# Single-block weight pieces and another order of scratch tiles in a fused mLSTM and SwiGLU kernel

## The chip, the cores and the metric

The kernel runs on one core of one Trainium2 chip. The metric is the time of one execution in microseconds (us), as the device reports it; the number that counts is the median of several runs. A core has a matmul engine (PE), a vector engine (DVE), a scalar engine for activations (ACT), a general engine (POOL), and SP, which here only issues DMAs. Each engine works through its own queue in order; semaphores hold an instruction until what it needs is there. DMAs that SP issues run on queue q1, those that POOL issues on queue q0; both move data through the same 16 DMA engines.

## What is computed

The reference has two steps. The first is an mLSTM cell over 768 time steps for 4 x 8 heads of 40 features; the second is a SwiGLU block on the 3072 x 320 matrix that the first gives.

```python
for t in range(S):
    m_new = np.maximum(f_gate[:, :, t] + m, i_gate[:, :, t])
    f_stab = np.exp(f_gate[:, :, t] + m - m_new); i_stab = np.exp(i_gate[:, :, t] - m_new)
    C = f_stab * C + i_stab * (v_t outer k_t);  n = f_stab * n + i_stab * k_t
    y[:, :, t] = sigmoid(o_gate) * (C @ q_t) / max(|n . q_t|, 1)
x = y as (3072, 320)
g = x @ w_gate;  out = (g * sigmoid(g) * (x @ w_val)) @ w_out
```

The three weight matrices come as 64-bit floats (320 x 1536, 320 x 1536 and 1536 x 320); all else is 32-bit. No engine of the kernel works in 64 bits, so the kernel turns the weights into 32-bit floats by integer operations on their two halves.

## The kernel before

**Tiling.** Time is cut into 6 groups of 128 steps (`g` from 0 to 5). For each group the recurrence is written in its chunked form: scores `k` against `q` (`sp`), weights from the gates (`w_sb`), the part from inside the chunk (`intra`), the part from the state (`inter`), and the update of the state (`add`, `C`). The group's output `x` (512 tokens of 320 features) is turned so that features lie on the partitions (`xT`), and the SwiGLU block follows for those tokens. The 1536 hidden features are 12 blocks of 128, so the two first matrices are 12 blocks each; block m of both is kept in `wgv_sb[:, m]`, gate weights on partitions 0 to 63 and value weights on partitions 64 to 127.

**Group 0** does a plain product for each block (`hidden`, L741 to L755: 40 matmuls of 512 columns at L749, then Silu on ACT and a multiplication on DVE at L755) and a plain output projection (`project_all`). **Groups 1 to 5** use a seven-product scheme for both matrix products: `gated` (L892 to L954) needs sums of weight blocks (`weight_sums`, L869 to L877, into the tiles `sw0` and `sw` and into `wgv_sb` itself) and sums of `xT` (`input_sums`); `project_seven` needs `wT`, `S1` and `S2`. The sums of weights are made once, in group 1.

**The weights come in while group 0 runs.** `PIECES` (L162) lists the loads: for `gv` (gate and value) or `o` (output matrix), the first block and the number of blocks. `piece_load` (L166 to L203) issues for a `gv` piece three DMAs: the gate half from SP, and the value half in two parts from POOL (`parts` 0, and 1 and 2; GATE and VALUE at L644). The 64-bit words land in a raw buffer: the pool `conv` has two buffers `raw` of 10,240 bytes per partition; some pieces take a home elsewhere that is free just then, the end of `h_sb` (`raw_h`, L645) or `wo_sb`. A piece that takes a `raw` buffer again waits until ACT has read the former piece. Then each block is converted (`convert`, L252): `scale` on ACT (two instructions, `top` at L225 and `low` at L227), `join` on DVE (L234, L235) and `rounded` on POOL or DVE (L242). Only then can PE use the block at L749.

**Before**, the `gv` pieces are: block 0, block 1, then pairs (2,3), (4,5), (6,7), (8,9), (10,11). Pieces 0 and 1 share one `raw` buffer; piece 2 lies in `raw_h`; piece 3 in the other `raw`; piece 5 in `wo_sb`. The tail of `h_sb` has held the first inputs (`dense`, L257). A memset of one element on POOL (L693) stands before piece 2, so that its DMAs wait for POOL alone.

**The order of the work** is written out by hand. L646 to L709 is the start: the first chunk's scores and weights, the turning of `x` (`seam`), the loads of pieces 0 to 3, and the conversion of blocks 0, 1 and 2. From L1011 on, lists say what follows which block of group 0: `ahead` (which block is converted while block m is multiplied), `slots` (what is issued after block m), `amid`, and `after` (what follows block m of the output projection of group 0). What stands in these lists is issued in that order on each engine's queue. The steps that matter here: in `slots`, 0 holds the loads of the next two pieces, 3 holds the load of the second group's `q` (`load_all` L1004, `load` L139, on SP), 5 the load of blocks 10 and 11 and of `v`; in `after`, 5 converts the last block, 6 and 7 make the weights of the third group (`weights_bias`, 16 exponentials each on ACT at L533) and weigh the values with them (`weigh_values`, L394 on POOL), 8 clears `x_sq` (POOL, L1008), 10 and 11 update the state (`do_decayed` on POOL at L418, `do_add` on PE at L409, `do_state` on DVE at L425) and turn `k` from a `raw` buffer (`early_squares(1)`, `turn_squares`, L373 on DVE). Group 1 then loads the next `k` into `x_sq` (`load_squares`, L367 on SP).

**Memory.** After group 0, the pools `early` and `conv` are closed (L1058) and the pool `late` takes their place: `wT` (11,520 bytes per partition), `S1` and `S2` (6,144 each) and `sw` (13,312), one behind the other in this order (L1066 to L1069). A late tile waits for the last use of the tiles that it lies over. By the sizes in the code, `early` fills about the first 6.6 KB of that space, then come the two `raw` buffers of 10,240 bytes, `top` and two `low`.

Of the kernel before, what the change touches and what calls it, by code (L numbers as in the profile page):

```python
# [9 lines left out]
F32 = mybir.dt.float32  # L10
BF16 = mybir.dt.bfloat16
I32 = mybir.dt.int32
U32 = mybir.dt.uint32
# [11 lines left out]
def kernel(  # L25
# [18 lines left out]
    nc = tc.nc  # L44
# [9 lines left out]
    NFC = DF // 128  # L54
# [3 lines left out]
    NKC = DM // HP  # L58
# [15 lines left out]
    def flat(t):  # L74
        return t.rearrange("p c t -> p (c t)")
# [44 lines left out]
    wo_sb = const.tile([128, NFC, DM], F32)  # L120
# [7 lines left out]
    x_sq = const.tile([128, B * NKC, L // SQ, SQ], F32)  # L128
# [30 lines left out]


    raws = {}
    PIECES = [("gv", 0, 1), ("gv", 1, 1)] + [("gv", m, 2) for m in range(2, NFC, 2)] + [("o", m, 4) for m in range(0, NFC, 4)]  # L162

    homes = {}

    def piece_load(p, home=None, parts=(0, 1, 2)):  # L166
        kind, m, n = PIECES[p]
        if kind == "gv":
            a, d = NKC, n * 128
            gate_w, val_w = (w[:, m * 128:(m + n) * 128].rearrange("(c p) f -> p c f", p=HP) for w in (moe_w_gate, moe_w_val))  # L170
            src = [(slice(0, HP), slice(0, NKC), gate_w), (slice(HP, 128), slice(0, NKC - 1), val_w[:, 1:]),
                   (slice(HP, 128), slice(NKC - 1, NKC), val_w[:, 0:1])]
        else:
            a, d = n, DM
            src = [(slice(0, 128), slice(0, n), moe_w_out[m * 128:(m + n) * 128].rearrange("(a p) d -> p a d", p=128))]
        if src[0][2].dtype == F32:
            for r, cs, w in [src[x] for x in parts if x < len(src)]:
                if kind == "o":
                    nc.sync.dma_start(out=wo_sb[r, m:m + n, :], in_=w)
                else:  # L180
                    for x in range(n):
                        nc.sync.dma_start(out=wgv_sb[r, m + x, cs], in_=w[:, :, ts(x, 128)])
            return
        if p in homes:
            raw = homes[p]
        else:
            if p < 2:
                if p == 0:
                    homes["raw"] = conv.tile([128, 4 * NKC * 128], U32, name="raw")
                raw = homes["raw"][:, ds(2 * p * a * d, 2 * a * d)]  # L190
            elif home is None:
                raw = conv.tile([128, 4 * NKC * 128], U32, name="raw")
            else:
                raw = home.rearrange("p a t -> p (a t)").bitcast(U32)
# [25 lines left out]
    def scale(j):  # L220
        if j in blocks:
            lo, hi, dst = blocks[j]
            a, d = hi.shape[1], hi.shape[2]
            top = conv.tile([128, NKC * 128], F32, name="top", bufs=1).rearrange("p (a d) -> p a d", a=a)
            nc.scalar.mul(top, hi.bitcast(F32), 2.0 ** -112)  # L225
# [335 lines left out]
    A, V, G = nc.scalar, nc.vector, nc.gpsimd  # L561
# [82 lines left out]
    GATE, VALUE = (0,), (1, 2)  # L644
    raw_h = h_sb[:, NH - NKC:]  # L645
# [38 lines left out]
    first_scores(1)  # L684
    first_gate(0, (G, G), A)
    piece_load(1, parts=VALUE)
    first_own(2)
    first_x(2)
    first_own(3)
    first_x(3)  # L690
    seam(0, 0, (A, A, A, A))
    first_gate(1, (G, V), V)
    nc.gpsimd.memset(raw_h[:, 0, 0:1], 0.0)  # L693
    piece_load(2, raw_h)
    piece_load(3)
    scale(0)
    ps0 = first_state(0, "gen")
    seam(0, 1, (V, A, A, A))
# [74 lines left out]
    KH = NFC // 2  # L773
# [230 lines left out]
    def load_all(dst, a, n, eng=nc.sync):  # L1004
        for P in range(2):
# [5 lines left out]
    on_vector = (9, 10, 11)  # L1011
    ahead = {0: [], 1: [3], 2: [4], 3: [5], 4: [6], 5: [7], 6: [8], 7: [9], 8: [10], 9: [11], 10: [], 11: []}
    slots = {
        0: [run(piece_load, 4), run(piece_load, 5, wo_sb)],
        1: [run(late_sums)],
        2: [run(late_maxima), run(M_store, G), run(load_all, k_sb, k, 1)],
        3: [run(late_decay), run(weights_load, 1), run(load_all, q_sb, q, 1)],
        4: [run(nc.scalar.activation, step1, step1, AF.Exp), run(decay_rows), run(cap_table)],
        5: [run(piece_load, 6), run(load_all, v_sb, v, 1), run(late_turns), run(decay)],
        6: [run(turn_one, P, k_sb, kT, (A, A)) for P in range(2)] + [run(weights_cap, 0), run(weights_cap, 1), run(piece_load, 7)],  # L1020
        7: [run(weights_sub, 1, 0), run(weights_sub, 1, 1), run(weights_exp, 0), run(weights_exp, 1), run(weigh_values, G, 0),
            run(weigh_values, G, 1)],
        8: [run(nc.gpsimd.memset, q_sb, 0.0), run(do_scores), run(piece_load, 8), run(load_all, o_sb, o_gate, 1)],
        9: [run(do_weigh, 0), run(do_weigh, 1), run(do_decayed, 2)],
        10: [run(do_add, 1, (0,)), run(rounded, 12), run(load_squares, q_sq, q, 2, (0,))],
        11: [run(do_intra, 0), run(do_inter, 1, 0), run(do_gather, 1, 0, False), run(piece_load, 9),
             run(load_squares, q_sq, q, 2, (1,))],
    }
    amid = {8: [run(turn_one, P, q_sb, qT, (A, A)) for P in range(2)], 11: [run(do_add, 1, (1,)), run(do_state, 2)]}
# [6 lines left out]
    def early_squares(part):  # L1036
# [11 lines left out]
        3: [run(do_divide, 1, 1), run(weights_cap, 0)],  # L1048
        4: [run(seam, 1, 0, (A, A, A, A)), run(convert, 16), run(weights_cap, 1), run(turn_squares, q_sq, qT)],
        5: [run(seam, 1, 1, (A, A, A, A)), run(convert, 17)],  # L1050
        6: [run(weights_bias, 2, 0), run(weigh_values, G, 0), run(input_sums, V)],
        7: [run(weights_bias, 2, 1), run(weigh_values, G, 1)],
        8: [run(nc.gpsimd.memset, x_sq, 0.0)],
        10: [run(do_decayed, 4), run(weight_sums, 0, V)],
        11: [run(do_add, 2), run(do_state, 4), run(early_squares, 1)],
    }
# [95 lines left out]
```

## Time and profile before

| | us |
|---|---|
| median of 3 runs (lowest, highest) | 514.84 (513.79, 519.25) |
| the profiled execution | 514.3 |
| its span, first to last instruction | 511.9 |
| PE busy | 502.5 (98% of the span) |
| DVE, POOL, ACT busy | 333.9, 261.9, 208.4 |
| DMA, mean over the span | 85 GB/s; 0 to 60 us: 192 GB/s |

The profile is of one execution. The page gives sums for each engine, a chain of work that ended last, and groups of instructions; the trace behind it can be asked for the waits of an engine, for all instructions in a stretch of time, and for the DMAs issued in a stretch. Times are from the start of the span. Group 0 takes about the first 126 us, each later group 78 us, and the last one ends without new recurrence work. Matmuls overlap in the pipeline, so the start of the next one says more than the end of the last.

### The profile page before, as it was taken

Reading aid. Unit: us, or ns where it says so; the run is one execution under the profiler, and the core shown is the slowest. Engines: PE = TensorE matmul, PEld = TensorE weight load, DVE = VectorE, ACT = ScalarE, POOL = GpSimd, SP = SyncE. Lnnn points to the kernel's source line nnn. Section 1 sums busy time; section 2 is a strip of 40 time slices with the busy share of each in tenths; the row PEclk is TensorE's granted clock in tenths of the full one; section 3 lists DMA queues with packets and bytes.
Section 4 is the critical chain, followed back from the end, with each engine's and each line's share of the span. In section 5 each row is a group of like instructions: output and inputs, shape, how many; then the busy total and the mean of one; then the engine's idle time right before and its main releaser. Section 6 shows DMA issues by size and latency. Waiting matters only on the chain.

```text
span 511.9 us, 15075 instructions
## 1 busy us (share of the span) xinstructions
PE 502.5 (98%) x6437; PEld 428.4 (84%) x6437; DVE 333.9 (65%) x543; ACT 208.4 (41%) x404; POOL 261.9 (51%) x289
## 2 busy tenths in 40 slices
PE   8989999999899999999999999999999999999997
PEld 4846655667788899888899988899988899988896
DVE  5869768887897777687466578467558554233421
ACT  3664784457342348312339321338321340223210
POOL 3624515366689653367643357652447650166710
PEclk9999999999999999999999999999999999999999
DMA  9999998797702992501992501992101200000001
GB/s 144 187 250 217 158 183 229 150 171 111 98 9 41 173 116 40 80 3 33 170 117 38 89 8 25 163 131 38 42 3 19 37 2 27 27 1 0 1 14 38
DMA packets 184378, 43.29 MB, mean 85 GB/s; under 512 B 172952, under 2 KB 179496, under 8 KB 183672
## 3 DMA queue, kind: packets, MB, share of 16 engines
q1 hardware_dynamic: 182948, 38.26, 46.9%
q0 software_dynamic: 1232, 4.02, 3.3%
q8 instruction: 50, 0.82, 0.7%
q14 instruction: 16, 0.13, 0.1%
q10 hardware_dynamic: 132, 0.07, 0.0%
HBM read 35.68 MB, written 4.01 MB: 78 GB/s over the span
## 4 chain that ended last, share of the span: by engine, by line
PE 85%; ACT 5%; DVE 3%; POOL 2%; issue 2%; DMA 1%; SPq 1%; DVEq 0%; ACTq 0%; POOLq 0%
PE gv_x L899 24%; PE o_ps L820 22%; PE gv_y L899 20%; PE gv_ps L749 6%; PE o_ps L766 3%; PE inter L432 2%; PE intra L441 2%; ACT w_sb L533 2%; PE add L409 1%; PE sp L383 1%; SPq L367 1%; DMA h_sb<-in_moe_w_val_dram 1%; ACT h_sb L582 1%; DVE wgv_sb L235 1%; PE burn L545 1%
## 5 line engine op out<-in xcount | busy, mean ns | idle before, releaser
L899 PE MATMUL gv_x<-xT,wgv_sb 64*128 64x256 f32 x720 | 89.3, 377 | 0.0
L899 PEld LDWEIGHTS gv_x<-xT,wgv_sb 64*128 64x128 f32 x720 | 69.7, 187 | 7.9 <-issue 0.2
L820 PE MATMUL o_ps<-wo_sb,h_sb 128*128 128x160 f32 x480 | 67.4, 300 | 0.0
L820 PEld LDWEIGHTS o_ps<-wo_sb,h_sb 128*128 128x128 f32 x480 | 65.6, 190 | 1.7 <-issue 1.7
L947 ACT ACTIVATE h_sb<-gv_x 128x256 f32<-128x256 f32 x30 | 11.5, 383 | 115.8 <-PE gv_x L899 115.8
L749 PE MATMUL gv_ps<-xT,wgv_sb 64*128 64x512 f32 x240 | 54.3, 597 | 1.5 <-DVE wgv_sb L242 1.4
L749 PEld LDWEIGHTS gv_ps<-xT,wgv_sb 64*128 64x128 f32 x240 | 28.2, 187 | 22.5 <-issue 15.2
L899 PE MATMUL gv_y<-xT,wgv_sb 64*128 64x256 f32 x360 | 44.0, 376 | 0.0
L899 PE MATMUL gv_y<-q_sb,wgv_sb 64*128 64x256 f32 x360 | 44.0, 376 | 0.0
L394 POOL TENSOR_TENSOR vw_sb<-v_sb,w_sb 128x656 f32<-128x656 f32 x10 | 14.6, 1462 | 53.8 <-ACT w_sb L533 40.5
L899 PEld LDWEIGHTS gv_y<-xT,wgv_sb 64*128 64x128 f32 x360 | 35.0, 187 | 3.9
L899 PEld LDWEIGHTS gv_y<-q_sb,wgv_sb 64*128 64x128 f32 x360 | 35.1, 187 | 3.9
L820 PE MATMUL o_ps<-wT,S 128*128 128x160 f32 x240 | 33.4, 299 | 0.0
L820 PEld LDWEIGHTS o_ps<-wT,S 128*128 128x128 f32 x240 | 32.9, 190 | 0.0
L899 PE MATMUL gv_x<-q_sb,sw 64*128 64x256 f32 x240 | 31.1, 377 | 1.3 <-POOL sw L873 1.3
L533 ACT ACTIVATE w_sb<-w_sb,g_T 128x64 f32<-128x64 f32 x128 | 31.0, 333 | 0.0
L920 POOL TENSOR_TENSOR h_sb<-x_sb 128x512 f32<-128x512 f32 x12 | 15.8, 1313 | 24.6 <-ACT x_sb L919 24.6
L940 POOL TENSOR_TENSOR tmp<-tmp 128x512 f32<-128x512 f32 x15 | 20.1, 1342 | 15.0 <-DVE tmp L939 15.0
L920 POOL TENSOR_TENSOR h_sb<-tmp 128x512 f32<-128x512 f32 x13 | 16.5, 1271 | 21.5 <-ACT tmp L919 21.5
L787 POOL TENSOR_TENSOR S<-h_sb 128x256 f32<-128x256 f32 x30 | 22.7, 756 | 9.2 <-DVE h_sb L920 7.3
L766 PE MATMUL o_ps<-wo_sb,h_sb 128*128 128x320 f32 x96 | 27.2, 438 | 0.0
L899 PE MATMUL gv_y<-q_sb,sw 64*128 64x256 f32 x200 | 27.0, 388 | 0.2 <-DVE tmp L917 0.2
(225 smaller groups left out, 987.2 us busy)
## 6 DMA issues: line engine op xcount, KB each, us to landing
w_sb<-M_dram SPq DMA_DIRECT2D x10, 512.0 KB, 7.2
v_sb<-in_v_dram SPq DMA_DIRECT2D x12, 320.0 KB, 6.2
o_sb<-in_o_gate_dram SPq DMA_DIRECT2D x12, 320.0 KB, 6.4
raw<-in_moe_w_out_dram SPq DMA_DIRECT2D x3, 1280.0 KB, 7.4
k_sb<-in_k_dram SPq DMA_DIRECT2D x10, 320.0 KB, 7.9
x_sq<-k_sb SPq DMA_DIRECT2D x64, 40.0 KB, 3.1
q_sb<-in_q_dram SPq DMA_DIRECT2D x32, 64.0 KB, 3.3
raw<-in_moe_w_gate_dram SPq DMA_DIRECT2D x3, 640.0 KB, 14.3
```

Source lines behind the costliest of these rows:

```text
L394: eng.tensor_tensor(vw_sb[:, heads(P)], v_sb[:, heads(P)], w_sb[:, heads(P), last].to_broadcast([128, UH, D1]), op=ALU.mult)
L432: nc.tensor.matmul(inter[two][half(i), a, :], lhsT=qT[feats(two), P * UA + a, half(i)], rhs=state(2 * n + i)[feats(two), P * UA + a, :], s ...
L441: nc.tensor.matmul(intra[i][half(c), a, :], lhsT=w_sb[half(i), h, :], rhs=v_sb[half(i), h, :], start=True, stop=True)
L533: nc.scalar.activation(w_sb[:, h], w_sb[:, h], AF.Exp, bias=g_T[:, n, h:h + 1], scale=-1.0)
L749: nc.tensor.matmul(ps[i], lhsT=wgv_sb[half(i), m, kc, :], rhs=x[half(i), kc, :], start=(kc == 0), stop=(kc == NKC - 1))
L766: nc.tensor.matmul(ps[u], lhsT=hid(g, m)[:, ts(u, L)], rhs=wo_sb[:, m, :], start=(m == 0), stop=(m == NFC - 1))
L787: eng.tensor_tensor(S1[:, k], lo[:, second_half], hi[:, second_half], op=ALU.add)
L820: nc.tensor.matmul(node[x][:, i], lhsT=lhs(k)[:, ts(i, L)], rhs=rhs(k), start=start and k == 0 and i == 0, stop=stop and k == KH - 1, skip ...
L899: nc.tensor.matmul(ps[:, i, cols], lhsT=lhs(c)[half(i)], rhs=rhs(c)[half(i)], start=start and c == 0, stop=stop and c == n - 1, skip_group ...
L920: (nc.vector if k == KH - 1 else nc.gpsimd).tensor_tensor(h_sb[:, 2 * k + 1], uw[:, 0], uw[:, 1], op=ALU.mult)
L940: nc.gpsimd.tensor_tensor(uw[:, :, second_half], uw[:, :, second_half], uw[:, :, first_half], op=ALU.add)
L947: nc.scalar.activation(h[:, first_half], x[:, 0, first_half], AF.Silu)
```

## The change

Four edits, with no change to what is computed.

1. Blocks 2 and 3 become pieces of one block each. Both lie in `raw_h`, in its two halves, each with a memset of one element of its own. The first memset moves up to stand behind the value request of block 1, ahead of `first_gate(1, ...)`; the second stands between the loads of the two pieces. Blocks 4 and 5 are thus piece 4, and the numbers of all later pieces grow by one. Each piece's request order is gate (SP), then value (POOL).
2. Of blocks 10 and 11, the gate half is still requested in slot 5; the value half moves to the head of slot 6. Slot 3, before both, holds the load of `q`.
3. In `late`, `sw` is allocated first and `wT` last.
4. The memset of `x_sq` moves from `after[8]` to the head of `after[6]`.

```diff
-    PIECES = [("gv", 0, 1), ("gv", 1, 1)] + [("gv", m, 2) for m in range(2, NFC, 2)] + [("o", m, 4) for m in range(0, NFC, 4)]
+    PIECES = [("gv", m, 1) for m in range(4)] + [("gv", m, 2) for m in range(4, NFC, 2)] + [("o", m, 4) for m in range(0, NFC, 4)]
...
-            if p < 2:
+            if p < 4:
                 if p == 0:
                     homes["raw"] = conv.tile([128, 4 * NKC * 128], U32, name="raw")
-                raw = homes["raw"][:, ds(2 * p * a * d, 2 * a * d)]
+                base = homes["raw"] if p < 2 else raw_h.rearrange("p m t -> p (m t)").bitcast(U32)
+                raw = base[:, ds(2 * (p % 2) * a * d, 2 * a * d)]
...
     piece_load(1, parts=VALUE)
+    nc.gpsimd.memset(raw_h[:, 0, 0:1], 0.0)
...
     first_gate(1, (G, V), V)
-    nc.gpsimd.memset(raw_h[:, 0, 0:1], 0.0)
-    piece_load(2, raw_h)
+    piece_load(2)
+    nc.gpsimd.memset(flat(raw_h)[:, 2 * NKC * 128:2 * NKC * 128 + 1], 0.0)
     piece_load(3)
+    piece_load(4)
...
-        0: [run(piece_load, 4), run(piece_load, 5, wo_sb)],
+        0: [run(piece_load, 5), run(piece_load, 6, wo_sb)],
...
-        5: [run(piece_load, 6), run(load_all, v_sb, v, 1), run(late_turns), run(decay)],
-        6: [run(turn_one, P, k_sb, kT, (A, A)) for P in range(2)] + [..., run(piece_load, 7)],
+        5: [run(piece_load, 7, parts=GATE), run(load_all, v_sb, v, 1), run(late_turns), run(decay)],
+        6: [run(piece_load, 7, parts=VALUE)] + [run(turn_one, P, k_sb, kT, (A, A)) for P in range(2)] + [..., run(piece_load, 8)],
...
-        6: [run(weights_bias, 2, 0), run(weigh_values, G, 0), run(input_sums, V)],
+        6: [run(nc.gpsimd.memset, x_sq, 0.0), run(weights_bias, 2, 0), run(weigh_values, G, 0), run(input_sums, V)],
         7: [run(weights_bias, 2, 1), run(weigh_values, G, 1)],
-        8: [run(nc.gpsimd.memset, x_sq, 0.0)],
...
-    wT = late.tile([128, 3, KH, NW], F32, name="wT")
+    sw = late.tile([128, 3 * KH - 5, 2, 128], F32, name="sw")
     S1 = late.tile([128, KH, TH], F32, name="S1")
     S2 = late.tile([128, KH, TH], F32, name="S2")
-    sw = late.tile([128, 3 * KH - 5, 2, 128], F32, name="sw")
+    wT = late.tile([128, 3, KH, NW], F32, name="wT")
```

The loads of the output matrix in slots 8 and 11 only take their new numbers (9 and 10).

More of the change, by code (lines that the diff above doesn't have):

```diff
@@ L1018 @@
         4: [run(nc.scalar.activation, step1, step1, AF.Exp), run(decay_rows), run(cap_table)],
-        5: [run(piece_load, 6), run(load_all, v_sb, v, 1), run(late_turns), run(decay)],
-        6: [run(turn_one, P, k_sb, kT, (A, A)) for P in range(2)] + [run(weights_cap, 0), run(weights_cap, 1), run(piece_load, 7)],
+        5: [run(piece_load, 7, parts=GATE), run(load_all, v_sb, v, 1), run(late_turns), run(decay)],
+        6: [run(piece_load, 7, parts=VALUE)] + [run(turn_one, P, k_sb, kT, (A, A)) for P in range(2)] + [run(weights_cap, 0), run(weights_cap, 1), run(piece_load, 8)],
         7: [run(weights_sub, 1, 0), run(weights_sub, 1, 1), run(weights_exp, 0), run(weights_exp, 1), run(weigh_values, G, 0),
             run(weigh_values, G, 1)],
-        8: [run(nc.gpsimd.memset, q_sb, 0.0), run(do_scores), run(piece_load, 8), run(load_all, o_sb, o_gate, 1)],
+        8: [run(nc.gpsimd.memset, q_sb, 0.0), run(do_scores), run(piece_load, 9), run(load_all, o_sb, o_gate, 1)],
         9: [run(do_weigh, 0), run(do_weigh, 1), run(do_decayed, 2)],
         10: [run(do_add, 1, (0,)), run(rounded, 12), run(load_squares, q_sq, q, 2, (0,))],
-        11: [run(do_intra, 0), run(do_inter, 1, 0), run(do_gather, 1, 0, False), run(piece_load, 9),
+        11: [run(do_intra, 0), run(do_inter, 1, 0), run(do_gather, 1, 0, False), run(piece_load, 10),
              run(load_squares, q_sq, q, 2, (1,))],
```

## The prediction

> **What bounds the kernel now.** I read the page's first two parts, then who waits for whom on the matmul engine, then the stretches of the timeline around those waits, then the DMA queues in the same stretches.
>
> ```profile
> span 511.9 us, 15075 instructions
> PE 502.5 (98%) x6437; PEld 428.4 (84%) x6437; DVE 333.9 (65%) x543; ACT 208.4 (41%) x404; POOL 261.9 (51%) x289
> PEclk9999999999999999999999999999999999999999
> ```
> PE (matmul) is busy 502.5 of 511.9 us at full granted clock. The change neither adds nor removes a matmul, so only PE's 9.4 us of idle time can move, and part of that lies at the start (1.2 us) and after the last matmul (511.9 - 508.0 = about 3.9 us).
>
> ```profile
> PE gv_ps L749 <- DVE wgv_sb L242: 1.4, 1, 1.4
> PE gv_x L899 <- POOL sw L873: 1.3, 1, 1.3
> PE add L409 <- DVE w_sb L390: 0.3, 1, 0.3
> PE tp_x L506 <- POOL x_sb L473: 0.2, 1, 0.2
> PE gv_y L899 <- DVE tmp L917: 0.2, 1, 0.2
> ```
> Columns: total us, times, longest. Two waits of over 1 us are left, both single events. After 139 us PE has no gap that a wait explains.
>
> First wait, block 2's weights (columns: start, length, engine, line, ... idle before):
>
> ```profile
> 34.86 0.79 ACT L225 ACTIVATE top<-h_sb 128x640 f32<-128x640 f32 x1 [3.83 <-DMA h_sb<-in_moe_w_val_dram]
> 37.17 0.82 DVE L242 CUSTOM_DVE_ANT_0 wgv_sb<-wgv_sb,low 128x1280 uint16<-128x1280 uint16 x1
> 38.14 7.21 PE L749 MATMUL gv_ps<-xT,wgv_sb 64*128 64x512 f32 x31 [1.40 <-DVE wgv_sb L242]
> ```
> ACT stands 3.83 us until the value half of blocks 2 and 3 has landed; PE is idle from 36.74 to 38.14. The DMA view of that stretch (last column: us from issue to landing):
>
> ```profile
> h_sb<-in_moe_w_gate_dram SPq DMA_DIRECT2D x1, 640.0 KB, 6.7
> raw<-in_moe_w_gate_dram SPq DMA_DIRECT2D x1, 640.0 KB, 14.3
> h_sb<-in_moe_w_val_dram POOLq DMA_DIRECT2D x1, 128.0 KB, 9.4
> ```
> The last value transfer is issued at 25.25 and lands 9.4 later, at 34.65. The gate half (24.32 + 6.7) is in by 31.0. The gate half of blocks 4 and 5 (24.97 + 14.3) lands at 39.3.
>
> Second wait, the first sums of the seven-product weights:
>
> ```profile
> 131.61 2.37 DVE L373 STREAM_TRANSPOSE kT<-raw 128x1024 f32<-128x1024 f32 x2
> 134.06 0.72 POOL L873 TENSOR_TENSOR sw<-wgv_sb 128x256 f32<-128x256 f32 x1 [3.65 <-DMA x_sq<-in_k_dram]
> 134.84 1.13 PE L899 MATMUL gv_x<-q_sb,sw 64*128 64x256 f32 x8 [1.25 <-POOL sw L873]
> ```
> The profile names a DMA as releaser of POOL, but POOL never reads x_sq here. DVE's transpose of `raw` ends at 133.98 and POOL starts 0.08 later. By the order of allocation, `sw` now begins 11,520 + 6,144 + 6,144 = 23,808 bytes into the late pool, and the second `raw` buffer (about 6.6 + 10.2 = 16.8 KB to 27.1 KB into the same space) lies under it. So I read it as: `sw` can't be written before `raw` has been turned.
>
> **Part 1, blocks 2 and 3 as pieces of one block.** The two blocks' bytes stay the same; one gate and two value DMAs become two and four, plus one memset (0.12 us, row L693). Moving the first memset ahead of POOL's L628 puts SP's gate request of block 2 at about 23.5 (now 24.32), and POOL's value requests at 24.4 (now 24.59). When do they land? Lower bound: the one-block value pieces of block 1 take 5.0 and 5.4 us, so 24.4 + 5.4 = 29.8. Upper bound: as long as now, 24.4 + 9.4 = 33.8. Queue 0, POOL's, carries 0.17 to 0.19 MB per us when busy (0.65 MB in 31 to 34.9, 0.95 in 34.9 to 40), so 0.33 MB less in front saves 1.8 us, and the earlier request 0.2: I take 32.6. From landing to PE's start the row gives 38.14 - 34.65 = 3.5 us, so PE needs the landing by 36.74 - 3.5 = 33.2. At 32.6 the whole **1.40 us** goes, with 0.6 to spare; at the upper bound 0.6 stays.
>
> What is late next? Block 3: PE wants it at 36.74 + 4.49 = 41.2, its conversion ends with POOL's rounding of 1.54, some 3.95 us from landing (0.80 + 0.47 + 0.83 + 1.54 and 0.3 of gaps), so 37.3 is enough. It follows block 2 by about 2 us. Covered. Block 4: PE wants it at 45.7, so it must land by 41.8, against 39.3 now. But SP now waits for the second memset, behind POOL's two value requests (1.19 us), so the gate request of blocks 4 and 5 leaves at about 26.5 instead of 24.97, behind two gate transfers of 1 KB rows instead of one of 2 KB rows. On DVE, `late_sums` (2.52 + 0.81) stands ahead of block 4's join, but that follows PE and comes earlier with it (join at about 41.4).
>
> Count packets on q1, SP's queue:
>
> ```profile
> q0 software_dynamic: 289, 0.95, 64.2%
> q1 hardware_dynamic: 287, 0.56, 39.7%
> ```
> (window 34.9 to 40: packets, MB, share). Both queues send equally many packets, 56 per us each; bytes follow packet size. Blocks 2 to 5 need 640 gate packets now and 960 after. Lower bound for the landing: equal bytes, 39.3. Upper: 320 more packets at 56 per us, 5.7 us, 45.0. Most of the added packets run before queue 0 is full, though: q1 sent 373 packets in 22 to 25, 124 per us, most of them under 2 KB. With 124 per us from 25 to 28.7 (460), then 500 at 55 per us (9.1), and the 2.5 us from last packet to landing that the present order shows, it lands at 40.3. I take 40.3: no wait, margin 1.5 us. This is the softest step.
>
> [...]
>
> **Part 2, value half of blocks 10 and 11 behind q.** Now requested at 58.40 to 59.74, it shares the engines with q's second half, issued at 54.64 and landed 14.9 later, 69.5; PE turns q at 69.40, in two halves, so nothing is to spare. With PE 1.4 us earlier, q would become the wait. Moved to the next slot, the request stands behind POOL's rounding of block 8 (60.08 + 1.53), leaves at about 60.3 on the shifted clock, and lands 7 to 8 us later, by 69; ACT wants block 10 at 73.50 - 1.4 = 72.1. Two POOL requests of 0.6 us move where POOL is idle anyway (12.9 us before L394). Cost 0, gain 0 by itself: it keeps part 1's 1.4. If q still lands at 69.5, up to 1.4 is lost.
>
> **Part 3, the order of the late tiles.** With `sw` first, it covers bytes 0 to 13,312: the small early tiles, done long before, and the first `raw` buffer, last read by ACT at 113.1. Then POOL's sums wait only for POOL's own order: `decayed` (last at 129.68 + 0.73 = 130.4). The first sum would be ready at 131.2, PE wants it at 133.59 (132.2 with the shift). The whole **1.25 us** goes. `wT` now lies over the second `raw`, but is first written some 20 us later. S1 begins at 13,312 and meets `raw` too; its first write is behind PE's second block pair, after the transpose. No instruction is added.
>
> **Part 4, x_sq cleared sooner.** The memset (2.23 us) moves on POOL from behind the second `weigh_values` to ahead of the first, where POOL waits 2.43 us for ACT between the two. `weigh_values` 1 moves from 119.31 to about 121.2, done 122.6, and 2 still starts at 123.1 behind ACT. Then `decayed` starts 2.2 us sooner, DVE's state (127.50) up to 2 us sooner, and the 0.17 us on L917 goes. SP's loads into x_sq gain 0.4 (its stores hold it until 126.34). On a shifted clock PE wants the second `weigh_values` by 123.9; ACT's chain (115.25 to 123.0) starts from PE's own transposes and shifts too. Bounds: 0.7 lost to 0.2 gained; I take **0.17** gained.
>
> **Sum.** 1.40 + 1.25 + 0.17 = 2.8 us. The profiled run took 514.3 (span 511.9 and 2.4 around it), so 511.5; the median of the runs, 514.84, is 0.5 above it and gives **512.0**.
>
> **Rivals.**
> (a) *Block 4's gate half pays* part of it back: landing between 41.8 and 44.6, wait 0 to 2.8, mean 1.4: about 513.4. Or one of parts 1 and 3 doesn't take (the releaser of `sw` was the DMA after all, or q still late): 514.84 - 1.4 = 513.4 as well. For it: margins of 1 to 1.5 us on estimates. Against: every shifted chain starts from PE.
> (b) *Slower*: block 4's gate half really follows the packet count. 45.0 makes PE wait 3.2 at block 4, which is 0.4 more than all gains: 515.2; if q1 also idles once more between two pieces (it sent 135 packets in 28 to 31, against 211 in 25 to 28) by 1.4, 516.6. It turns slower from a landing of 44.6 on. Against it: the first third of the packets has the engines nearly alone.
> (c) *Nothing moves*: the waits only change their names and come back at the next place, 514.8. Against it: PE has no other wait on a DMA-paced chain past 139.
>
> **Chances.** Forecast 0.57 (511.0 to 512.8), (a) 0.22, (b) 0.09, (c) 0.12. Range 510.6 to 515.4: from the forecast's lower edge, through (a) and (c), to the lower end of (b). Over 1%, about what a measurement of this kernel can tell from no change, is 5.1 us: all removable idle time of PE is less, so faster by more needs a disturbed median, 0.03; slower by more needs twice (b), 0.04.
>
> **What would show it.** Right: no PE wait on L242 near 37 and none on `sw` near 132; ACT's `top<-h_sb` before 33.2 for block 2; POOL's first L873 right after `decayed`; q landed well before 68. Wrong: a PE wait on POOL's L242 near 46 (block 4), ACT's `top<-raw` after 42, POOL still starting `sw` with the end of L373, or a wait of PE's `add` near 124 on `vw_sb`.

## The result and the profile after

The changed kernel takes 510.99 us (median of 22 runs, 508.96 to 519.61); the kernel before, measured beside it, took 514.05 us (22 runs). The ratio is 0.9941, 95% interval 0.992 to 0.9962: 2.0 to 4.1 us faster. (The ratios here and below are not the quotients of the two medians and differ a little from them.) The profiled execution took 509.04 us and is near the lower end of the runs, so its span shows more than the median does: 4.7 us less than before. The page of the changed kernel, its first part:

```profile
span 507.2 us, 15081 instructions
PE 501.3 (99%) x6437; PEld 425.8 (84%) x6437; DVE 332.8 (66%) x543; ACT 208.2 (41%) x404; POOL 260.2 (51%) x292
```

PE now leaves 5.9 us of the span, against 9.4. Who PE waited for (columns: total us, times, longest), all that is left of the list:

```profile
PE burn L546 <- DVE warm L276: 1.2, 1, 1.2
PE first_y L614 <- DVE h_sb L604: 0.3, 1, 0.3
PE tp_kq L351 <- ACT h_sb L583: 0.2, 1, 0.2
```

The 1.4 at block 2 and the 1.3 on `sw` are gone, and nothing took their place in this execution. (Line numbers after the change are 1 higher up to about L690, then 3 higher; experiments without part 1 have the old ones.) Where the 4.7 us came from, by the starts of the same PE instructions in both profiles (a block of group 0 is 20 matmuls in the trace, 240 for the 12 blocks):

| PE instruction | before | after | gained so far |
|---|---|---|---|
| first block of group 0 | 27.76 | 27.48 | 0.28 |
| block 2 | 38.14 | 36.24 | 1.90 |
| turns of the gate sums (`tp_g`) | 56.01 | 53.53 | 2.48 |
| block 11 | 85.51 | 82.64 | 2.87 |
| output block 6, behind the last turns of `x` | 111.45 | 108.26 | 3.19 |
| `add` of the third group | 124.56 | 121.66 | 2.90 |
| first product on `sw` | 134.84 | 130.65 | 4.19 |
| the product that follows it on `tmp` | 139.47 | 134.93 | 4.54 |
| end of the span | 511.9 | 507.2 | 4.7 |

Block 2's conversion and the loads behind it, on the changed kernel's timeline (columns: start, length, engine, line, operation, output and input, idle before):

```profile
30.84 0.80 ACT L226 ACTIVATE top<-h_sb 128x640 f32<-128x640 f32 x1
38.41 0.79 ACT L226 ACTIVATE top<-raw 128x640 f32<-128x640 f32 x1 [1.38 <-DMA raw<-in_moe_w_gate_dram]
71.03 0.83 ACT L226 ACTIVATE top<-raw 128x640 f32<-128x640 f32 x1
```
These are blocks 2, 4 and 10. ACT finds block 2 ready and starts it at 30.84 (34.86 before); block 4's gate half is in at 38.4; block 10 starts without a wait at 71.03.

The same timeline where DVE updates the state and POOL makes the first sums (POOL has cleared `x_sq` from 116.84 on):

```profile
123.30 4.10 DVE L426 TENSOR_TENSOR C<-C,add 40x328 f32<-40x328 f32 x8 [0.63 <-PE add L410]
...
125.48 0.74 POOL L419 TENSOR_TENSOR C<-C,dec 128x328 f32<-128x328 f32 x1 [0.30 <-DVE C L426]
126.17 0.73 POOL L876 TENSOR_TENSOR sw<-wgv_sb 128x256 f32<-128x256 f32 x1
...
127.41 2.37 DVE L374 STREAM_TRANSPOSE kT<-raw 128x1024 f32<-128x1024 f32 x2
```
POOL's sum into `sw` follows the last decay at once and no longer waits for the transpose. But the transpose itself also starts 4.20 us sooner (131.61 before), 1.3 more than PE's shift at that place. Which of the two made the wait go, the two profiles can't say; the runs below do.

### The profile page after: what moved, and what is told of

Its sections match the earlier page's. It is cut to its first block, busy times and chain, and to the rows that moved or that the text cites. A ratio compares the mean times of both kernels' runs of the same rounds, so it can differ in the third digit from the quotient of the medians.

```text
span 507.2 us, 15081 instructions
## 1 busy us (share of the span) xinstructions
PE 501.3 (99%) x6437; PEld 425.8 (84%) x6437; DVE 332.8 (66%) x543; ACT 208.2 (41%) x404; POOL 260.2 (51%) x292
## 4 chain that ended last, share of the span: by engine, by line
PE 92%; DMA 3%; SPq 2%; ACT 1%; DVE 1%; issue 0%; DVEq 0%; ACTq 0%
PE gv_x L902 26%; PE o_ps L823 23%; PE gv_y L902 21%; PE o_ps L769 5%; PE gv_ps L752 5%; PE inter L433 2%; PE sp L384 2%; DMA raw<-in_moe_w_val_dram 2%; PE intra L442 2%; PE add L410 2%; DMA M_dram<-M_sb 1%; SPq L139 1%; ACT h_sb L583 1%; PE sp L600 1%; PE burn L546 1%; PE tp_x L507 1%
## 5 line engine op out<-in xcount | busy, mean ns | idle before, releaser
L752 PEld LDWEIGHTS gv_ps<-xT,wgv_sb 64*128 64x128 f32 x240 | 25.6, 187 | 23.1 <-issue 20.3
L769 PE MATMUL o_ps<-wo_sb,h_sb 128*128 128x320 f32 x96 | 27.4, 439 | 0.0
L942 DVE TENSOR_TENSOR tmp<-tmp,gv_y 128x1024 f32<-128x1024 f32 x15 | 18.1, 1205 | 13.8 <-PE gv_y L902 12.0
## 6 DMA issues: line engine op xcount, KB each, us to landing
w_sb<-M_dram SPq DMA_DIRECT2D x10, 512.0 KB, 6.7
```

What stands on the lines that cost most here:

```text
L752: nc.tensor.matmul(ps[i], lhsT=wgv_sb[half(i), m, kc, :], rhs=x[half(i), kc, :], start=(kc == 0), stop=(kc == NKC - 1))
L769: nc.tensor.matmul(ps[u], lhsT=hid(g, m)[:, ts(u, L)], rhs=wo_sb[:, m, :], start=(m == 0), stop=(m == NFC - 1))
L942: nc.vector.tensor_tensor(uw, uw, y, op=ALU.add)
```

## Experiments

### Which part brings the gain

**Part 4 alone.** The kernel before, with the memset of `x_sq` moved.

```diff
-        6: [run(weights_bias, 2, 0), run(weigh_values, G, 0), run(input_sums, V)],
+        6: [run(nc.gpsimd.memset, x_sq, 0.0), run(weights_bias, 2, 0), run(weigh_values, G, 0), run(input_sums, V)],
-        8: [run(nc.gpsimd.memset, x_sq, 0.0)],
```

> Only the memset of x_sq moved ahead. Theory of the prediction (parts 3 and 4 are separate, 1.25 and 0.17): PE still waits over 1 us for sw, span 0.2 us shorter. Rival (they are two ways to one gain): DVE's state starts 2 us sooner, its transpose of raw ends near 132, POOL's first sum is ready near 133, PE does not wait for sw, span 1.2 to 1.5 us shorter.

Measured: 512.73 us, ratio 0.9967 (0.9953 to 0.9982). POOL's first sum, on its timeline:

```profile
125.40 4.10 DVE L425 TENSOR_TENSOR C<-C,add 40x328 f32<-40x328 f32 x8 [0.63 <-POOL C L418]
...
129.51 2.37 DVE L373 STREAM_TRANSPOSE kT<-raw 128x1024 f32<-128x1024 f32 x2
...
131.96 0.73 POOL L873 TENSOR_TENSOR sw<-wgv_sb 128x256 f32<-128x256 f32 x1 [3.64 <-DMA x_sq<-in_k_dram]
```
`sw` still lies over `raw`, and POOL still waits 3.64 us, but the transpose (named by the order of the rows, as before; the profile names the DMA) ends at 131.88 in place of 133.98, because DVE's state starts at 125.40 in place of 127.50. That is soon enough: PE's wait on `sw` is gone from the list. Part 4 alone is worth about 1.7 us (0.9 to 2.4), ten times the 0.17 that the prediction gave it. The rival in the expectation came true.

**Part 3 alone.** The kernel before, with `sw` allocated first and `wT` last.

```diff
-    wT = late.tile([128, 3, KH, NW], F32, name="wT")
+    sw = late.tile([128, 3 * KH - 5, 2, 128], F32, name="sw")
...
-    sw = late.tile([128, 3 * KH - 5, 2, 128], F32, name="sw")
+    wT = late.tile([128, 3, KH, NW], F32, name="wT")
```

> Only the order of the late tiles. Theory (the transpose of the raw buffer held sw, not the DMA named): POOL's first sum starts right after its last decay, near 130.5, PE does not wait for sw, span 1.2 to 1.4 us shorter than before. Rival (the DMA into x_sq held it): POOL's sum still starts near 134 and nothing changes.

Measured: 514.5 us, ratio 0.9999 (0.998 to 1.0018). Its timeline and its PE waits:

```profile
131.58 0.73 POOL L873 TENSOR_TENSOR sw<-wgv_sb 128x256 f32<-128x256 f32 x1
...
132.82 2.37 DVE L373 STREAM_TRANSPOSE kT<-raw 128x1024 f32<-128x1024 f32 x2
```
```profile
PE gv_y L899 <- DVE tmp L939: 1.0, 1, 1.0
```
The reading of the releaser holds: with `sw` elsewhere POOL's sum starts 1.2 us ahead of the transpose, so the transpose and not the DMA that the profile named had held it. But the state and the transpose keep their places in DVE's queue, and the next thing that DVE owes PE, the sum into `tmp` one product later, is now late by 1.0. Most of the wait changed its name: 1.25 on `sw` and 0.17 on `tmp` before, 0.97 on `tmp` now. The interval allows 1 us either way; the profile shows where it went. This execution also lost 0.8 before q's turns and 0.9 at an `add` near 85, long before any late tile is written, so its span says nothing on part 3.

**All but part 3.**

> The changed kernel with the late tiles in their old order. Theory of the prediction: POOL waits for the transpose of raw again, PE waits about 1.25 us for sw, span 508.5 against 507.2 of the changed kernel. Rival (with the memset moved the order no longer matters): the transpose ends near 129.8, the first sum is ready at 130.6 when PE wants it (130.65), so 0 to 0.3 us lost, span 507.2 to 507.5.

Measured (the diff is part 3 taken back): 510.49 us, ratio 0.9921 (0.9899 to 0.9944). No wait on `sw` in the list. With part 4 in place, part 3 adds nothing that these runs can see. One other wait is there:

```profile
PE gv_ps L752 <- DVE wgv_sb L243: 1.5, 1, 1.5
```
That is block 10, and it comes back below.

**Part 1 alone.** Single pieces for blocks 2 and 3 (the first half of the change's diff), the rest as before.

> Blocks 2 and 3 as own pieces; the value half of blocks 10 and 11 is still asked for in slot 5, the late tiles and the memset of x_sq stay as before. Theory (part 1 gains, part 2 protects it): no PE wait at block 2, PE reaches block 6 some 2.2 us sooner than before (54.9 instead of 57.1), but then PE waits 1 to 1.5 us for q, whose second half lands near 68 to 69 while PE wants it near 67.5; the wait on sw stays at 1.25. Span 510.5 to 511. Rival (q is asked for sooner with everything else, so part 2 is not needed): no PE wait at the turning of q, span 509.5.

Measured: 513.25 us, ratio 0.9987 (0.9962 to 1.0013). Its PE waits:

```profile
PE add L410 <- DVE w_sb L391: 2.3, 2, 1.9
PE gv_x L902 <- POOL sw L876: 1.4, 1, 1.4
```
No wait at block 2, as forecast; the wait of 1 to 1.5 us for q that the expectation gave to part 1 without part 2 is 0.24. The interval includes no gain at all. In this execution PE stands 1.94 us at an `add` near 84, where the kernel before stood 0.32. It is not the usual one: it took 516.96 us, third longest of twelve, and nine of the twelve took 511.4 to 513.9 with a mean granted clock of 0.999 or 1.0, against 0.997 here. The timeline of that stretch:

```profile
77.14 1.31 POOL L395 TENSOR_TENSOR vw_sb<-v_sb,w_sb 128x656 f32<-128x656 f32 x1 [0.81 <-ACT top L226]
77.54 3.00 DVE L235 TENSOR_SCALAR wgv_sb<-top 128x640 uint32<-128x640 uint32 x1
78.39 1.81 POOL L1011 MEMSET q_sb<- 128x2048 f32 x1
```
DVE's first step for block 11 takes 3.00 us in place of 0.48. It began 0.40 us after the start of POOL's work on the values and ended 0.3 us after POOL's memset, so it lies beside two POOL instructions in a row. No run here takes the POOL work away to prove that POOL is the cause.

**Parts 1 and 2.** The same with the value half of blocks 10 and 11 in the later slot.

```diff
-        5: [run(piece_load, 7), run(load_all, v_sb, v, 1), run(late_turns), run(decay)],
-        6: [run(turn_one, P, k_sb, kT, (A, A)) for P in range(2)] + [...],
+        5: [run(piece_load, 7, parts=GATE), run(load_all, v_sb, v, 1), run(late_turns), run(decay)],
+        6: [run(piece_load, 7, parts=VALUE)] + [run(turn_one, P, k_sb, kT, (A, A)) for P in range(2)] + [...],
```

> Parts 1 and 2 alone; late tiles and memset as before. Theory of the prediction (part 2 keeps the 1.4 that part 1 gains, since q lands sooner): 1.0 to 1.4 us faster than part 1 alone (513.25), so near 512. Rival (part 1 alone made PE wait only 0.24 us for q, and what part 2 saves there it takes from the gate half of block 10 by flowing beside it): within 0.5 us of part 1 alone, 513 to 513.5, and the wait on sw of 1.4 still there.

Measured: 513.78 us, ratio 0.9966 (0.9935 to 0.9996). In its profile PE does not wait for q, ACT waits 1.58 us for block 10's gate half, and the `add` is late by 1.93 again, behind a DVE step of 2.73 us of the same kind; this execution (515.52 us) was the second longest of twelve. The two theories differ by 1 us, less than the intervals of these runs allow to tell; the wait of 1.4 on `sw` is still there, since parts 3 and 4 are left out. Parts 1 and 2 (0.9966) and part 4 (0.9967) multiply to 0.9933, inside the interval of the whole change (0.992 to 0.9962).

**The change without part 2.** The diff above taken back in the changed kernel.

> The changed kernel without part 2: the value half of blocks 10 and 11 is asked for with their gate half, beside q and ahead of it on the engines, as in the kernel before. The prediction's theory (part 2 costs and gains nothing by itself): PE's waits as in the changed kernel, 0.2 to 0.3 us for q's turns at most, ratio 0.992 to 0.994. Rival (the value half takes bytes from q while PE comes to q's turns): a wait of 0.5 to 0.9 us of PE or of its turns for q_sb at about 65 us, as the kernel with part 3 alone showed (0.76), ratio 0.994 to 0.9955. Second rival (the value half in front leaves the gate half less to share with later, so block 10 is safe): no wait at block 10, clock 1.0 throughout, ratio 0.990 to 0.992.

Measured: 511.75 us, ratio 0.9953 (0.9927 to 0.9978). Its PE waits:

```profile
PE add L410 <- DVE w_sb L391: 0.9, 2, 0.6
PE tp_kq L351 <- DMA q_sb<-in_q_dram: 0.8, 1, 0.8
```
Block 10 is in time (ACT starts it at 71.47 without a wait), and q is late by 0.8. The first rival came true, in the wait and in the ratio; of the second, block 10 is safe in this execution but the ratio is not what it said, and the mean granted clock is 0.997 or less in five of the twelve runs. In this profile, then, part 2 takes a wait off q and puts the risk on block 10. In the median the two can't be told apart.

### The limit that the prediction called its softest step

**Blocks 4 and 5 asked for one place later**, behind blocks 6 and 7.

```diff
-    piece_load(4)
...
-        0: [run(piece_load, 5), run(piece_load, 6, wo_sb)],
+        0: [run(piece_load, 5), run(piece_load, 4), run(piece_load, 6, wo_sb)],
```

> The changed kernel, with blocks 4 and 5 asked for one place later on the queues, behind blocks 6 and 7. This measures the limit that the prediction called its softest step: PE needs block 4's gate half by about 41.8, and in the changed kernel it lands at 38.4. Asked for second, it should land about where that of blocks 6 and 7 lands now, 43 to 44.3. Theory (limit 41.8, then 1 us per us): ACT waits for it and PE stands 1.2 to 2.5 us at block 4, the median is 512.3 to 513.8, ratio 0.9955 to 0.9975; where PE stands 2 us or more, 3.4 us at a granted clock of 0.5 follow at once and the span is 1.7 us longer still. Rival (the limit is later than worked out, or the gate half lands at 41 or sooner since the two requests are served together): no wait at block 4, ratio 0.992 to 0.994.

Measured: 516.91 us, ratio 1.0044 (1.0019 to 1.0068). ACT's timeline, PE's waits, and two windows of 2 us after the wait (columns: us, then busy time of PE, PEld, DVE, ACT, POOL with their instructions, granted clock, DMA share, GB/s):

```profile
45.90 0.78 ACT L226 ACTIVATE top<-raw 128x640 f32<-128x640 f32 x1 [7.14 <-DMA raw<-in_moe_w_gate_dram]
```
```profile
PE gv_ps L751 <- POOL wgv_sb L243: 3.1, 1, 3.1
```
```profile
50.00:52.00 2.00, 2.00 (x8) 0.89 (x8) 1.97 (x3) 0.09 (x1) 0.35 (x1) 0.66 1.14 162
52.00:54.00 2.00, 2.00 (x6) 0.80 (x6) 2.00 (x3) 1.01 (x2) 1.54 (x2) 0.50 0.29 49
```
The gate half landed later than I expected (45.9, not 44.3), and the wait follows it. The limit is the time at which PE comes to block 4 less the time from ACT's start to PE's. The second is 3.91 here, against 3.95 reckoned. PE came to block 4 at 46.74, 1.0 later than the 45.7 reckoned with, after a gap of 1.04 us near 25 us that the profile puts down to issue. So the limit was 42.8 in this execution, 41.8 on the forecast's clock, and PE waited 3.07 for a landing at 45.9. A second point: in the run of single blocks 10 and 11 (below) the gate half came at 41.87 and PE began block 4 3.95 later, after a wait of 0.25, which gives 41.6. Both terms of the limit near 41.8 thus hold. That PE's wait equals what the landing is past the limit is arithmetic, not a finding. After the wait the clock falls to 0.5 (0.66 and 0.50 over the two rows are about 3.4 us at 0.5), which costs 1.7 more. The median is 3 us above what I expected (512.3 to 513.8). The profiled execution is 7.0 us longer than the first of the changed kernel; the standing (3.1), the clock (1.7) and the gap (1.0) make 5.8 of it, and the rest is open.

### What still moves between executions of the changed kernel

**The changed kernel once more.**

> The changed kernel unaltered, as a second profile of it beside the next three. Theory (what varies from one execution to the next is when the gate half of blocks 10 and 11 lands): median near 511, and if this profile is longer than the 507.2 us of the first, the difference sits at PE's block 10 or at the `add` behind it, with ACT's `top<-raw` waiting for `in_moe_w_gate` near 71 to 74. Rival: the difference is spread over the whole span.

Measured: 511.83 us, ratio 0.9921 (0.9891 to 0.995); the profiled execution has a span of 511.0, 3.8 more than the first one. ACT's timeline, PE's waits, and windows:

```profile
74.02 0.79 ACT L226 ACTIVATE top<-raw 128x640 f32<-128x640 f32 x1 [2.39 <-DMA raw<-in_moe_w_gate_dram]
```
```profile
PE gv_ps L752 <- DVE wgv_sb L243: 2.0, 1, 2.0
```
```profile
80.00:82.00 2.00, 2.00 (x8) 1.38 (x9) 1.83 (x3) 0.07 (x1) 2.00 (x3) 0.65 0.90 233
82.00:84.00 2.00, 2.00 (x6) 1.22 (x5) 2.00 (x3) 1.40 (x2) 0.44 (x1) 0.50 1.03 412
```
PE's starts are 0.47 us later than in the first profile up to block 9 and 4.62 later at the `add` behind block 10, so 4.15 us are lost at this one place (0.8 of it comes back further on): block 10's gate half lands at 74.0 in place of 71.0 or sooner, PE stands 1.98 us, and 3.4 us at half clock (1.7 us lost) come behind it.

Most of the later landing is a later request. It leaves SP at 57.4 in the first profile and at 59.8 here. Ahead of it on SP stand `w_sb`, which waits for the store of M (2.3 us in the first profile), and q. The store leaves POOL at 44.85 and 46.72; it waits for a DVE scan (L333; 1.90 us in the first profile), which stands in DVE's queue behind the conversion of block 4, and block 4's gate half came at 38.4 and 40.9. The run with blocks 4 and 5 asked for late (above) bears this chain out: there block 4's gate half came at 45.9, the store left at 51.65 and the request for block 10's at 60.7. So what is late at block 4 without costing PE anything can cost it at block 10.

The mean granted clock of each run says how often the fall of the clock comes: 3.4 us at half speed make 0.997 of the mean, and 0.997 or less is found in 6 of the 34 runs of the changed kernel. Most of the runs that are longer than the first profile therefore owe it to something else; a wait at block 10 below 2 us, like the 1.5 of all but part 3, may be part of it, but no profile here shows how much.

**The gate half of blocks 10 and 11 ahead of `w_sb` and q.**

```diff
-        3: [run(late_decay), run(weights_load, 1), run(load_all, q_sb, q, 1)],
+        3: [run(late_decay), run(piece_load, 7, parts=GATE), run(weights_load, 1), run(load_all, q_sb, q, 1)],
-        5: [run(piece_load, 7, parts=GATE), run(load_all, v_sb, v, 1), run(late_turns), run(decay)],
+        5: [run(load_all, v_sb, v, 1), run(late_turns), run(decay)],
```

> The changed kernel, but the gate half of blocks 10 and 11 is asked for in slot 3, ahead of the weights and q, instead of slot 5. Theory (its landing behind q limits PE at block 10 in most executions): ACT never waits for it near 71 to 74, it lands near 56, w_sb and q land some 2 us later (q near 67, still ahead of PE at 67 to 68, or 0 to 0.5 us of wait); median 1 to 2 us below the changed kernel, 509 to 510, and less spread. Rival (PE's wait only moves to q): median unchanged, a wait of over 1 us at the turning of q.

Measured: 512.86 us, ratio 0.994 (0.9909 to 0.997).

```profile
PE tp_kq L351 <- DMA q_sb<-in_q_dram: 3.1, 1, 3.1
```
The gate half lands at 57.4, far too soon, and q pays: PE stands 3.1 us before q's turns, as the rival said. No gain.

**The same, with the third group's first cap to `w_sb` put behind the conversion of block 16.** This was to take away the small wait of DVE at 107.8 (L530, 1.96 us for `w_sb`), which makes output block 8 late by 0.28 in the changed kernel.

```diff
-        3: [run(do_divide, 1, 1), run(weights_cap, 0)],
-        4: [run(seam, 1, 0, (A, A, A, A)), run(convert, 16), run(weights_cap, 1), run(turn_squares, q_sq, qT)],
+        3: [run(do_divide, 1, 1)],
+        4: [run(seam, 1, 0, (A, A, A, A)), run(convert, 16), run(weights_cap, 0), run(weights_cap, 1), run(turn_squares, q_sq, qT)],
```

> As e7, and the first half of the cap on the third group's weights goes behind the conversion of block 16, on DVE. In the changed kernel DVE stood 1.96 us before that cap for w_sb to land, block 16 was ready at 112.8 and PE lost 0.28 us at output block 8. Theory (that wait is the next one on PE's path): 0.3 us of e7's span goes at that place, up to 1 us in executions where w_sb lands late; median 0.2 to 0.6 below e7. Rival (0.28 us is all there ever is, and it comes back as DVE's work slides): equal to e7 within 0.3.

The e7 of the text is the experiment just above. Measured: 513.57 us, ratio 0.9951 (0.9922 to 0.9981). q is late again by 3.2, and now block 17 is late: PE stands 0.7 at L769 for POOL's rounding of it. Both caps, one behind the other, stand on DVE ahead of its conversion. The wait moved by one block and grew from 0.28 to 0.7; the theory falls.

**Blocks 10 and 11 as pieces of one block**, in the same places of the queues.

```diff
-    PIECES = [("gv", m, 1) for m in range(4)] + [("gv", m, 2) for m in range(4, NFC, 2)] + ...
+    PIECES = [("gv", m, 1) for m in range(4)] + [("gv", m, 2) for m in range(4, 10, 2)] + [("gv", 10, 1), ("gv", 11, 1)] + ...
...
```

> The changed kernel, with blocks 10 and 11 also as pieces of their own (gate 10, gate 11 in turn on SP behind q, value 10 and value 11 in turn on POOL), so that block 10's gate half no longer has to land together with block 11's. Theory (block 10's gate half, asked for behind q, is what is left of the changed kernel's losses: its landing at 71.0 in one execution and 74.0 in the other makes ACT wait 0 or 2.39 us and PE 0 or 1.98 us, and 2 us of PE standing bring 3.4 us at a clock of 0.5): half the bytes land about 2.5 us sooner (two gate halves of 655 KB land about 5 us apart on that queue: 38.4, about 43.6, 48.9), so ACT waits at most 0.2 us at block 10, PE does not wait there, no slice of 80 to 90 us runs at 0.5, the span is 507.0 to 507.6 and the median 509.0 to 510.5, ratio about 0.990. Rival 1 (what holds the gate half up are the bytes of q and v that share the engines, not its own size): ACT still waits 1 to 2.4 us, the median stays at 511 to 512, ratio 0.992 to 0.994. Rival 2 (rows of 1 KB in place of 2 KB, and two more issues on each queue, make v or block 12 late): a new wait of 0.5 us or more at another place, and a median at or over 511.5.

Measured: 511.16 us, ratio 0.9944 (0.9916 to 0.9971).

```profile
73.62 0.78 ACT L226 ACTIVATE top<-raw 128x640 f32<-128x640 f32 x1 [1.13 <-DMA raw<-in_moe_w_gate_dram]
```
The theory of size falls for the most part. Block 10's gate half, with half the bytes, still lands at 73.6, and block 11's at 74.7, 1.1 later. The request left late here (60.2, behind a block 4 at 41.9); from request to landing it took 13.4 us, against 14.2 to 14.6 for the undivided half where its landing shows (the changed kernel again, parts 1 and 2, all but part 3). So half the bytes save about 1 us and not 2.5. The rest I put down to the bytes of q and v beside it (the DMA share from 60 to 72 us is 1.06 to 1.55 in this profile); no run takes them away. PE waits 0.2 to 0.3 us at three places in this execution, and the median is that of the changed kernel.

**q ahead of `w_sb`.**

```diff
-        2: [run(late_maxima), run(M_store, G), run(load_all, k_sb, k, 1)],
-        3: [run(late_decay), run(weights_load, 1), run(load_all, q_sb, q, 1)],
+        2: [run(late_maxima), run(M_store, G), run(load_all, k_sb, k, 1), run(load_all, q_sb, q, 1)],
+        3: [run(late_decay), run(weights_load, 1)],
```

> The changed kernel, with q of the second span asked for on SP right behind k, ahead of w_sb, in place of behind w_sb. w_sb cannot be asked for before the store of M lands (50.6), while SP is through with k at 48.3, so q's bytes would move from 48.3 on, in a stretch in which the 16 DMA engines are not full (share 0.73 at 52 to 56 us in the execution with single pieces). The same bytes then stand ahead of block 10's gate half, but begun 1.5 to 2.5 us sooner. Theory (the gate half of block 10 is late because of what is queued ahead of it on SP): it lands 1.5 to 2.5 us sooner, at 69 to 72 in place of 71 to 74; ACT does not wait for it, PE stands neither there nor at q's turns, clock 1.0 throughout, span 507.0 to 507.8, median 509.0 to 510.5, ratio 0.988 to 0.992. Rival 1 (w_sb now lands at 60 to 63, and DVE, which adds the cap to it at 60.5 and works in order, stands up to 2.5 us with the conversion of block 9 behind it): a wait for DVE's or POOL's conversion of a gv block, or for w_sb, of 0.5 to 2 us, ratio 0.993 to 0.996. Rival 2 (the bytes of v beside it, not the queue ahead, set when the gate half lands): it lands at 71 to 74 as before, ratio 0.992 to 0.994.

Measured: 515.56 us, ratio 1.0024 (0.9992 to 1.0056). Its timeline on DVE, and its PE waits:

```profile
64.01 2.36 DVE L530 TENSOR_TENSOR w_sb<-w_sb,cap 128x1024 f32<-128x1024 f32 x2 [3.29 <-DMA w_sb<-M_dram]
```
```profile
PE sp L384 <- ACT qT L143: 3.0, 1, 3.0
```
Rival 1, and more than its price: `w_sb` lands at about 64, DVE adds the cap 3.5 us later than in the changed kernel, and ACT's exponentials of it, which stand in ACT's queue ahead of the copies of q's turns, follow. PE stands 3.0 us, and the clock is at 0.5 from about 73 to 79.7; the mean clock, 0.993 or less in eleven of the twelve runs, says that this is the rule here.

So `w_sb`, q and block 10's gate half share 50 to 74 us (DMA share 0.93 to 1.38 there, in stretches of 6 us of the changed kernel's first profile), and putting the gate half or q first made another late. Of the four orders tried, none beats that of the changed kernel, and no kernel tried here is shown to be faster than it.

## Why the prediction was right, and where it was not

The forecast was 512.0 from 514.84, a ratio of 0.9945; measured were 510.99 and 0.9941. The absolute difference of 1.0 is mostly that of the kernel before between the two sets of runs (514.84 and 514.05). The size is right; two of its four terms are not, and what it left out goes both ways. That the total came out is in part luck: parts 3 and 4 were wrong one by one and right as a sum, and losses and gains that it had no term for lie between the profile's 4.7 us and the median's 3.0.

**Part 1, right in the wait, 1.40 forecast and 1.62 measured** in the profile (1.90 less the 0.28 of the start). Block 2's value half landed at 30.30 in the first profile, near the lower bound of 29.8, and at 32.6, the estimate, in the second. That a single piece doesn't wait behind the other block's value bytes is my reading. The runs of part 1 alone can't tell its gain from none; those of parts 1 and 2 give 0.2 to 3.3 us.

**Block 4's gate half**, estimated at 40.3 between 39.3 and 45.0, landed at 38.4 in the first execution, under the lower bound, and ACT began on it at 40.9 in the second and at 41.9 in three experiments with the same loads. The limit of 41.8 was right to 0.2. The choice of 40.3 was thus in the middle of what happens, and the margin of 1.5 is all used in some executions, at 0.25 of PE's time. The slower rival rested on both queues sending equally many packets. The queues of the changed kernel in 28 to 31 us (columns: packets, MB, share):

```profile
q1 hardware_dynamic: 341, 0.35, 56.7%
q0 software_dynamic: 116, 0.34, 50.8%
```
The counts of packets are 3 to 1, those of bytes equal. SP's queue sent 114 packets per us here (338 in the 3 us before), where the working had 55 from 28.7 us on; that is the term which put the landing too late for this execution. The equal counts of before (289 and 287) were no rule for this stretch, though 34.9 to 40 has them again after the change (287 and 274), and 320 more gate packets didn't delay the landing by 5.7 us. What sets the two counts, no run shows.

**Part 2, cost 0 and gain 0: not told apart from it**, but the step looked at the wrong half. It showed that the value half lands in time (forecast by 69, landed at 69.3 and 70.0) and that q does too (no wait before q's turns in the first profile, 0.3 in the second: right). The gate half, behind q on SP, is what lands last, 71 to 74.4, with ACT wanting it at about 71.5. So the shift that part 1 earns is paid back there in part of the executions: 1.5 us in the profile of all but part 3, 2.0 in the second profile, where the fall of the clock costs 1.7 more. The prediction's first rival had this mechanism (a gate half that comes after its limit), at block 4 instead of block 10.

**Part 3, 1.25 forecast: wrong as a cause.** The step that failed is "the whole 1.25 us goes" for the order of the late tiles. Its reading of the releaser was right, but nothing was asked about DVE's next debt to PE; alone, part 3 turned 1.25 on `sw` and 0.17 on `tmp` into 0.97 on `tmp`, and its ratio was 0.9999.

**Part 4, 0.17 forecast: mis-sized.** The text had the right movement, "DVE's state up to 2 us sooner" (measured 2.10), and counted only the small wait on L917. The transpose is behind the state on DVE, so it comes 2.1 sooner too, which is more than the 1.25 that PE lacked. Part 4 is worth 1.7 alone, and it takes the wait with or without part 3. The sum of parts 3 and 4, 1.42, came out right by luck, because either was enough for the wait on `sw`, and part 4 for what follows.

**Left out.** Above the forecast: 1.3 us between block 2 and 111 us. 0.6 of it lies before 56 us and has no line among PE's waits; I read it as waits too short to show under matmuls that overlap in the profile (the last one before the turns of the gate sums ends at 53.60, and these start at 53.53), which no run tested. The rest comes at the `add` near 84 and at the last turns of `x` near 111, where the prediction's own list shows waits of 0.3 and 0.2 that the sum gave nothing for. Below it: block 10, and 0.28 at output block 8, where PE now comes before POOL's rounding at 112.8. In the profiled execution the gain is 4.7, in the median 3.0.

## What to carry to other kernels

Before a wait is credited to the edit that removes its releaser, ask what the same engine owes the waiting one next: an edit that brings the engine's whole queue forward (a memset of POOL moved past two instructions, so that DVE's state starts 2.1 us sooner) removed both waits, one that freed a single tile removed one and made the next. When an early wait goes, list every transfer that PE meets afterwards and ask whether it is tied to PE's progress or to a queue of its own; the ones on their own queue set the new limit. Ask too what that queue waits for: here a load that came late without a wait of PE held a store, and the store held the next load. Where three loads share a full stretch of DMA, giving one of them the front may only choose which one is late.

## What the runs showed of the hardware

**The clock after a short stand.** In six profiles the granted clock fell to 0.5 behind a stand of PE: for 3.4 us after 1.98 us (the changed kernel again), after 1.93 and 1.94 with a further 0.32 close behind (parts 1 and 2; part 1), after 3.07 (blocks 4 and 5 later) and after 3.2 (the cap behind block 16), and for 6.8 us after 3.0 (q ahead of `w_sb`). It stayed at 1.0 after 1.40 (before) and 1.5 (all but part 3), and once after 3.1 (gate half sooner), though the mean clock is 0.997 or less in nine of the other eleven runs of that kernel. Why that stand of 3.1 passed, no run shows. In the second profile of the changed kernel a wait of 1.98 cost 3.7 us with the 1.7 lost behind it.

**DVE steps beside POOL.** The same conversion step of 128x640 takes 0.46 to 0.50 us where POOL is idle, and 1.55 (the changed kernel), 2.73 (part 3; parts 1 and 2) and 3.00 (part 1) where POOL had begun its work on the values just before or was still at it; in the steps of 2.73 and 3.00 POOL's memset followed within the step. Which of them meets the other differs from execution to execution. In these three profiles with 2.73 or 3.00 at block 11, the longest wait of PE's `add` was 0.9 to 1.9 us (0.3 before).

**The same load takes up to 3 us more.** With the same requests in front, block 4's gate half took 12.5 us from request to landing in the first profile (38.4) and 15.2 to 15.4 in three others (41.9). Block 10's came at 71 to 74.4, but there the request itself left SP at 57.4 to 59.8. Margins below that size on a transfer are chances, not covers.
